# One core, HGRN2 outer-product attention followed by an activation MLP: the work of all engines put in a new order

## The chip, the cores and the metric

The kernel runs on one core of a Trainium2 chip. A core has a matrix engine (PE), a vector engine (DVE), an activation engine (ACT), a general engine (POOL), and queues that start DMAs (SP issues nearly all of them here). Each engine runs its own instructions strictly in the order in which they stand in its queue, and waits on semaphores for what the others deliver. The metric is the device time of one execution in microseconds, the median of several runs.

## The reference

The first half is a gated linear recurrence over 768 positions for 4 batches of 8 heads with 48 channels; the second half is a two-layer MLP with the activation h · erf(softplus(h)).

```
f = 1.0 / (1.0 + np.exp(-f_logit))
for t in range(S):
    state = f[:, :, t, :, None] * state + np.einsum('bhd,bhe->bhde', k[:, :, t], v[:, :, t])
    y[:, :, t] = np.einsum('bhd,bhde->bhe', q[:, :, t], state)
x = y.transpose(0, 2, 1, 3).reshape(B * S, H * D)      # 3072 x 384
h = x @ w_in                                           # 384 -> 2048
sp = np.maximum(h, 0.0) + np.log1p(np.exp(-np.abs(h)))
g = h * erf(sp)
out = g @ w_out                                        # 2048 -> 384
```

## The kernel before

The recurrence is cut into 24 chunks of 128 positions (6 for each batch), each in two halves of 64. Two chunks make a block of 256 tokens, so that the MLP runs over 12 blocks, each with 4 groups of 512 hidden channels.

A program of 1770 short tokens in the string STEPS says in which order all of this is issued. A token is a step's name, its numbers, sometimes the engine (a, v or g for ACT, DVE or POOL), and behind an @ the buffer that it takes. For chunk g: `f q k v` load; `cl ex ln` make log decays (DVE, ACT, ACT); `d` sums them (PE); `e` turns sums into decays (ACT, two instructions); `qd kd` scale q and k (DVE); `tq tk` or `tx` transpose both on PE; `aq ak` copy the transposes out; `ds` and `sc` are PE's state products and scores; `m` and `s` mask the scores (on DVE, or for chunks 3 to 9 by a copy on ACT and a select on POOL); `st` updates the running state on DVE for each half; `sp` copies the state to the operand of the next half; `y` is PE's output product for each half, and `x` copies the chunk to the block's input xT. For block b and group i: `h` is half a group's hidden product (6 matmuls of 128x256), `c` copies the group out of PSUM, `ae ax aw ah` are ACT's four functions, `at au am` DVE's three products, `ka kb kt` (ACT, DVE, DVE) split the result in three parts, and `o` is 4 matmuls of 128x384 that project one part. `ro rp so` gather a block's rows and store them.

The weights arrive in 16 pieces (`p`) and are rounded by seven steps each (`r`, step 0 on ACT and six on DVE); pieces 0 to 7 are w_in, and a hidden half p needs piece p. The four groups of w_out are split in parts by `kc` (ACT), `ku kD kM` (DVE). Block 0 is projected with plain w_out; the parts are needed from block 1 on, and lie in the memory that block 0's activations used.

Within an engine the order is that of the tokens and of nothing else. PSUM is four pairs of banks (@0 to @3 on PE's steps), and the activations share 13 slots of [128, 1024] (@0 to @12). A step that takes a buffer waits until its last reader is done. In the listings below a name such as pair_3385 is one use of a PSUM pair, early_m_110 the second half of plain w_out, form_c, form_d and form_m its parts, h, e, x, ga, gb, gs the activation slots.

The change touches STEPS, `form_d`, `copy_x`, `copy_h`, and the tiles called early, which were all made at the start. The engine of `sp`, `ak` and `v` was already a letter in the token; `x`, `c` and `kD` had a fixed one.

Of the kernel before, what the change touches and what calls it, by code (L numbers as in the profile page):

```python
# [79 lines left out]
def kernel(  # L80
# [133 lines left out]
    early = {n: parts.tile([P, PAIR], FP32, name=f"early_{n}", tag=n) for n in ("c0", "c1", "d0", "d1", "m0", "m1")}  # L214
    formed = {}

    def plain(ft, n=1):
        pair, at = divmod(ft * d_model, PAIR)
        return early[f"m{pair}"][:, at : at + n * d_model].rearrange("p (a w) -> p a w", w=d_model)
# [67 lines left out]
    def load_piece(i):  # L287
# [7 lines left out]
        raw = None if wpe == 1 else early[home[:2]][:, at : at + 2 * PIECE].bitcast(U32)  # L295
# [51 lines left out]
    def flat_form(t, gi):  # L347
        return form(t, gi).rearrange("p j c -> p (j c)")
# [261 lines left out]
    def copy_x(g):  # L610
        blk, j = divmod(g, CPB)
        if blk not in xTs:
            xTs[blk] = work.tile([P, n_k, TB], FP32, name="xT", tag="xT")
        nc.scalar.copy(out=xTs[blk][:, :, j * P : (j + 1) * P], in_=yts[g][:])
# [130 lines left out]
    def pads(_):  # L745
# [6 lines left out]
        f0 v0 k0 q0 f1 in0 ms0 zb0@0 p0 q1 cl0 ex0 k1 ln0 v0_0_0g v1 z5 d0@1 v0_0_1g f2 v0_1_1g  # L752
        e0 v0_1_0g p1 v2 kd0 z3 to0@1 qd0 p2 tk0@2 ta0 k2 cl1 tq0 ex1 q2 ak0a ds0 f3 aq0 st0 p3
        st1 sp0g ln1 v3 z2 sc0 r0_0 d1@2 p4 sp1g m0_0_1 m0_1_1 p5 e1 m0_0_0 r0_1 f4 z1 y0_0@3
        r0_2 to1@2 qd1 m0_1_0 kd1 z2 tq1@1 v1_0_0g ta1 r0_3 v1_0_1g q3 y0_1 v1_1_0g aq1 r0_4 k3
        tk1 v1_1_1g cl2 r0_5 f5 x0 ds1 ex2 r0_6 ak1a ln2 z2 sc1 st2 d2@1 st3 r1_0 sp2g p6 m1_0_0
        e2 p7 m1_1_1 sp3g m1_0_1 v4 m1_1_0 z3 y1_0@3 r1_1 v2_0_1g y1_1 r1_2 v2_1_0g to2@2 r1_3
        v2_1_1g x1 w3 v2_0_0g ta2 h0_0@0 r1_4 r2_0 r1_5 r2_1 kd2 r2_2 k4 tk2@3 qd2 r1_6 q4 ds2
        ak2a tq2 cl3 v5 st4 ex3 h0_1 r2_3 ln3 sp4g aq2 r2_4 r2_5 r3_0 r2_6 sc2 c0_0 r3_1 d3@3
        m2_0_0 ax0_0@0 m2_1_1 h0_2@0 f6 m2_0_1 m2_1_0 r3_2 r3_3 e3 r3_4 f7 y2_0@1 r3_5 r4_0 y2_1  # L760
        r3_6 to3@3 ae0_0@1 ta3 x2 st5 h0_3 r5_0 w4 r4_1 sp5g r4_2 aw0_0@2 r5_1 r4_3 qd3 c0_1
        r4_4 tq3@2 q5 kd3 ae0_1@3 r4_5 ds3 k5 tk3 aq3 v6 st6 cl4 sp6g ak3a r4_6 ex4 sc3 r5_2
        h0_4@2 p8 r5_3 r5_4 m3_0_0 m3_0_1 r5_5 m3_1_0 m3_1_1 s3_0 r6_0 r5_6 s3_1 ln4 st7 h0_5 p9
        r6_1 r7_0 sp7g r6_2 r6_3 r7_1 y3_0@3 r7_2 c0_2 r7_3 y3_1 d4@0 x3 w5 r6_4 d5@2 e4 r6_5
        h1_0@3 e5 r7_4 qd4 kd4 q6 r7_5 k6 tx4@2 r6_6 f8 to4@0 aq4 to5@1 r7_6 h1_1 ak4v ta4 ta5
        cl6 p10 qd5 ex6 p11 at0_0 ds4 sc4 c1_0@4 q7 v7 st8 m4_0_0 h0_6@3 m4_0_1 kd5 f9 sp8g
        m4_1_0 st9 m4_1_1 ln6 au0_0 s4_0 ax0_1@0 s4_1 h0_7 k7 sp9g r8_0 at0_1 ah0_0 y4_1@0 r8_1
        r8_2 c0_3 y4_0 r8_3 tx5@2 ms6 w6 x4 aw0_1@0 r8_4 h1_2@0 ak5v aq5 r8_5 r8_6 ax0_2@2 ds5
        am0_0 p12 r9_0 sc5 d6@2 v8 m5_0_0 h1_3 st10 m5_0_1 m5_1_0 r9_1 m5_1_1 sp10g e6 r9_2 r9_3
        s5_1 ae0_2@1 tt6 qd6 h1_4@2 r10_0 kd6 r9_4 c1_1@5 s5_0 r10_1 r10_2 r10_3 y5_0@0 r10_4  # L770
        y5_1 r10_5 tx6@1 x5 r9_5 w7 h1_5 aq6 ak6v r9_6 r10_6 p13 h1_6@1 c1_2@6 au0_1 k8 p14
        r11_0 at0_2 aw0_2@0 q8 r11_1 h1_7 ax0_3@2 r11_2 r11_3 ah0_1 r11_4 r11_5 r12_0 sc6@2
        am0_1 c1_3@7 ds6 d7@0 v9 o0_0_0@3 m6_0_0 st12 m6_0_1 f10 r12_1 m6_1_0 sp12g m6_1_1 r12_2
        e7 r12_3 s6_0 ae0_3@3 qd7 s6_1 h2_0@0 kd7 tt7 st13 r12_4 sp13g r12_5 r11_6 y6_0@2 y6_1
        r12_6 h2_1 x6 au0_2 r13_0 r14_0 r13_1 p15 r13_2 ah0_2 w8 tx7@2 r14_1 r14_2 c2_0@0 o0_0_1
        r14_3 aq7 ak7v q9 am0_2 aw0_3@8 k9 h2_2@2 r13_3 f11 ae1_0@1 r13_4 r14_4 r13_5 ds7@0
        r14_5 sc7 v10 h2_3 st14 m7_0_0 m7_0_1 at0_3 m7_1_0 sp14g m7_1_1 s7_0 au0_3 ax1_0@2
        o0_1_0 s7_1 r13_6 c2_1@9 r14_6 ah0_3 cl8 r15_0 am0_3 y7_0@2 ex8 y7_1 r15_1 o0_1_1 w9
        r15_2 r15_3 x7 r15_4 ln8 r15_5 aw1_0@3 h2_4@2 r15_6 at1_0 ae1_1@8 au1_0 o0_2_0 ax1_1@2
        st15 cl10 ah1_0 sp15g at1_1 aw1_1@3 h2_5 am1_0 aw1_2@2 au1_1 ka1_0@1 d8@0 ah1_1 o0_2_1  # L780
# [6 lines left out]
        kD3 ax2_0@12 kb1_2@10 au1_3 o1_2_0_0 c3_0@6 o1_2_0_1 kM2 ah1_3 o1_2_1_0 f12 h3_2@2
        aw2_0@11 kt1_2@5 qd9 kd9 q11 am1_3 h3_3 k11 at2_0 ae2_1@2 ka1_3@3 au2_0 tx9@3 ax2_1@12
        o1_2_0_2 kM3 o1_2_1_1 aq9 o1_2_1_2 ak9v ah2_0 o1_3_0_0 kb1_3@5 ds9@3 aw2_1@10 sc9 v12
        st18 o1_3_1_0 c3_1@7 kt1_3@11 sp18g o1_3_0_1 m9_0_0 o1_3_1_1 m9_0_1 am2_0 m9_1_0  # L790
        o1_3_0_2 m9_1_1 s9_0 ro1 o1_3_1_2 at2_1 ka2_0@8 s9_1 h3_4@1 au2_1 ae2_2@11 ax2_2@12
        kb2_0@5 h3_5 ah2_1 kt2_0@10 aw2_2@0 am2_1 rp1 y9_0@2 ae2_3@2 y9_1 at2_2 so1 c3_2@3
# [12 lines left out]
        ah3_3 f15 h4_3 ae4_0@9 am3_3 aw4_0@7 at4_0 ka3_3@4 sc11@2 au4_0 ds11 c4_1@12 o3_2_0_0
        v14 m11_0_0 o3_2_0_1 ah4_0 m11_0_1 o3_2_0_2 m11_1_0 m11_1_1 ax4_1@7 y11_0@1 st22
        o3_2_1_0 kb3_3@10 sp22g ae4_1@11 o3_2_1_1 kt3_3@0 o3_2_1_2 aw4_1@5 y11_1 am4_0 o3_3_0_0
        x11 w13 o3_3_0_1 at4_1 ka4_0@9 h4_4@1 au4_1 kb4_0@7 ah4_1 h4_5 kt4_0@5 am4_1 o3_3_0_2
        cl14 c4_2@1 o3_3_1_0 ax4_2@11 o3_3_1_1 h4_6@1 ae4_2@4 ro3 at4_2 ka4_1@10 h4_7 aw4_2@11
        kb4_1@3 ex14 au4_2 d12@3 o3_3_1_2 c4_3@11 o4_0_0_0@2 kt4_1@0 e12 o4_0_0_1 ah4_2  # L810
        o4_0_0_2@1 rp3 tt12 o4_0_1_0 qd12 h5_0@0 kd12 ax4_3@9 am4_2 ae4_3@12 h5_1 ka4_2@4 at4_3
# [332 lines left out]
```

## Time and profile before

| | us |
|---|---|
| median of 3 runs | 616.17 (615.49 to 618.18) |
| the profiled execution | 618.82 |
| its span | 617.1 |
| PE busy | 584.0 (95%) |
| DVE busy | 481.7 (78%) |
| ACT busy | 444.8 (72%) |
| POOL busy | 86.5 (14%) |

The span runs from the first to the last instruction of the profiled execution, which is 2.65 us longer than the median. Two stages differ. Up to about 200 us the weights are rounded while the first chunks and blocks run, and DVE is the busiest engine; from there PE is busy almost without a break to its last matmul at 609 us. A row of the timeline gives the start, the time, the engine, the line, the operation with its output and inputs, the number of instructions merged, and in brackets the idle time ahead of it with what ended it. PE's times within a row of several matmuls overlap with those of the next row, so that PE's pace is read from start to start. A matmul of 32-bit operands shows as two records.

### The profile page before, as it was taken

Reading aid. Unit: us, or ns where it says so; the run is one execution under the profiler, and the core shown is the slowest. Engines: PE = TensorE matmul, PEld = TensorE weight load, DVE = VectorE, ACT = ScalarE, POOL = GpSimd, SP = SyncE. Lnnn points to the kernel's source line nnn. Section 1 sums busy time; section 2 is a strip of 40 time slices with the busy share of each in tenths; the row PEclk is TensorE's granted clock in tenths of the full one; section 3 lists DMA queues with packets and bytes.
Section 4 is the critical chain, followed back from the end, with each engine's and each line's share of the span. In section 5 each row is a group of like instructions: output and inputs, shape, how many; then the busy total and the mean of one; then the engine's idle time right before and its main releaser. Section 6 shows DMA issues by size and latency. Waiting matters only on the chain.

```text
span 617.1 us, 14290 instructions
## 1 busy us (share of the span) xinstructions
PE 584.0 (95%) x5885; PEld 501.3 (81%) x5885; DVE 481.7 (78%) x603; ACT 444.8 (72%) x524; POOL 86.5 (14%) x133
## 2 busy tenths in 40 slices
PE   7897989899799999999999999999999999999995
PEld 6676867666588798888888888888888888889994
DVE  4989879999968989966867678569567778566783
ACT  4476586679768898879685786786898584575881
POOL 3203230223503200200001101100100101200000
PEclk9988989999989999999999999999999999999998
DMA  9986666411122112402132125113522121010000
GB/s 236 268 200 155 164 147 155 109 34 17 49 35 45 41 32 34 83 9 54 25 80 51 27 44 86 28 40 53 105 51 40 29 53 14 2 27 1 0 27 30
DMA packets 153095, 41.38 MB, mean 67 GB/s; under 512 B 144832, under 2 KB 147904, under 8 KB 153024
## 3 DMA queue, kind: packets, MB, share of 16 engines
q1 hardware_dynamic: 150944, 40.01, 29.8%
q8 instruction: 48, 0.79, 0.6%
q10 hardware_dynamic: 2080, 0.39, 0.3%
q14 instruction: 23, 0.19, 0.1%
HBM read 35.59 MB, written 4.72 MB: 65 GB/s over the span
## 4 chain that ended last, share of the span: by engine, by line
PE 75%; DVE 13%; ACT 5%; issue 3%; POOL 1%; SPq 1%; DMA 0%; DVEq 0%; ACTq 0%; POOLq 0%
PE pair L627 33%; PE pair L703 28%; PE pair L604 4%; PE pair L541 2%; DVE e L176 2%; PE pair L480 2%; PE pair L553 2%; DVE qA L578 1%; PE pair L427 1%; PE pair L561 1%; DVE early_m L341 1%; DVE state L522 1%; ACT qA L576 1%; ACT x L171 1%; PE pair L471 1%
## 5 line engine op out<-in xcount | busy, mean ns | idle before, releaser
L627 PE MATMUL pair<-xT,w_in_sb 128*128 128x256 f32 x1152 | 266.7, 387 | 7.4 <-ACT kd L436 2.5
L627 PEld LDWEIGHTS pair<-xT,w_in_sb 128*128 128x128 f32 x1152 | 220.1, 193 | 41.9 <-ACT kd L436 4.0
L176 DVE SCALAR_TENSOR_TENSOR e<-x,e 128x1024 f32<-128x1024 f32 x96 | 117.3, 1224 | 29.2 <-ACT e L168 19.5
L132 POOL COPY sv<-state 48x192 f32<-48x192 f32 x88 | 61.5, 699 | 457.8 <-DVE state L523 327.8
L171 ACT ACTIVATE x<-h,serf_bias 128x1024 f32<-128x1024 f32 x88 | 100.3, 1145 | 5.1 <-PE pair L703 1.6
L703 PE MATMUL pair<-form_c,ga 128*128 128x384 f32 x352 | 81.1, 352 | 1.3 <-DVE rows L717 1.3
L703 PE MATMUL pair<-form_m,gs 128*128 128x384 f32 x352 | 80.0, 350 | 0.0
L703 PE MATMUL pair<-form_d,gb 128*128 128x384 f32 x352 | 77.2, 341 | 0.0
L655 ACT ACTIVATE e<-e 128x1024 f32<-128x1024 f32 x48 | 50.7, 1057 | 28.5 <-DVE e L176 28.1
L659 DVE TENSOR_TENSOR h<-h,e 128x1024 f32<-128x1024 f32 x44 | 54.0, 1228 | 19.9 <-ACT e L655 19.7
L671 DVE TENSOR_TENSOR gb<-h,ga 128x1024 fp32r<-128x1024 f32 x44 | 54.5, 1239 | 14.2 <-ACT ga L666 10.4
L703 PEld LDWEIGHTS pair<-form_m,gs 128*128 128x128 f32 x352 | 62.4, 190 | 3.5 <-issue 2.1
L634 ACT COPY h<-pair 128x1024 f32<-128x1024 f32 x44 | 44.4, 1009 | 28.7 <-PE pair L627 25.9
L703 PEld LDWEIGHTS pair<-form_c,ga 128*128 128x128 f32 x352 | 60.5, 188 | 5.2 <-issue 2.3
L703 PEld LDWEIGHTS pair<-form_d,gb 128*128 128x128 f32 x352 | 61.9, 188 | 1.4 <-DVE gs L678 0.3
L666 ACT ACTIVATE ga<-h 128x1024 fp32r<-128x1024 f32 x44 | 46.3, 1053 | 20.0 <-DVE h L659 19.6
L678 DVE SCALAR_TENSOR_TENSOR gs<-ga,gb 128x1024 fp32r<-128x1024 f32 x44 | 54.1, 1230 | 3.5 <-PE pair L703 1.9
L168 ACT ACTIVATE e<-h 128x1024 f32<-128x1024 f32 x44 | 46.1, 1048 | 6.0 <-DVE h L659 3.0
L604 PEld LDWEIGHTS pair<-qA,sv 128*32 128x32 f32 x1536 | 26.1, 112 | 18.8 <-issue 6.4
L604 PE MATMUL pair<-qA,sv 128*32 128x64 f32 x1536 | 32.1, 225 | 9.6 <-POOL qA L585 5.1
L494 ACT COPY qA<-pair 64x512 f32<-64x512 f32 x48 | 27.8, 580 | 10.4 <-PE pair L480 5.0
L522 DVE TENSOR_TENSOR state<-pair,state 112x192 f32<-112x192 f32 x40 | 14.2, 355 | 24.1 <-PE pair L553 16.1
(92 smaller groups left out, 572.6 us busy)
## 6 DMA issues: line engine op xcount, KB each, us to landing
early_d<-in_moe_w_out_dram SPq DMA_DIRECT2D x8, 768.0 KB, 4.9
qn<-in_q_dram SPq DMA_DIRECT2D x24, 192.0 KB, 3.2
out_dram<-rows SPq DMA_DIRECT2D x12, 384.0 KB, 2.5
kn<-in_k_dram SPq DMA_DIRECT2D x23, 192.0 KB, 3.3
vt<-in_v_dram SPq DMA_DIRECT2D x23, 192.0 KB, 3.4
sv<-in_v_dram SPq DMA_DIRECT2D x84, 48.0 KB, 2.5
lt<-in_f_logit_dram SPq DMA_DIRECT2D x80, 48.0 KB, 2.4
early_m<-in_moe_w_in_dram SPq DMA_DIRECT2D x4, 768.0 KB, 6.2
```

The lines of the kernel that those rows point to most:

```text
L132: (engine.copy if engine is nc.scalar else engine.tensor_copy)(out=out, in_=in_)
L168: nc.scalar.activation(out=dst[:], in_=h, func=AF.Exp)
L171: nc.scalar.activation(out=dst[:], in_=h, func=AF.Tanh, bias=serf_bias[:, i : i + 1], scale=SERF_KAB[i][0])
L176: nc.vector.scalar_tensor_tensor(out=e[:], in0=x[:], scalar=SERF_KAB[i][2], in1=e[:], op0=ALU.add, op1=ALU.mult)
L604: nc.tensor.matmul(y[M * i : M * (i + 1), kt, half(c)], lhsT=sv[:, r, c, a, o : o + M], rhs=qA[:, r, a, half(c)], start=(first and n == 0) ...
L627: nc.tensor.matmul(hts[blk, gi][:, j, :], lhsT=w_in_sb[:, kt, ft * P : (ft + 1) * P], rhs=xTs[blk][:, kt, :], start=(kt == 0), stop=(kt == ...
L655: nc.scalar.activation(out=e[:], in_=e[:], func=AF.Tanh, scale=SERF_C)
L659: nc.vector.tensor_tensor(out=h, in0=h, in1=es.pop((blk, gi))[:], op=ALU.mult)
L666: nc.scalar.activation(out=gps_[blk, gi][0][:], in_=hs[blk, gi], func=AF.Copy, scale=KAPPA)
L671: nc.vector.tensor_tensor(out=gps_[blk, gi][1][:], in0=hs[blk, gi], in1=a[:].bitcast(FP32), op=ALU.subtract)
L678: nc.vector.scalar_tensor_tensor(out=gps_[blk, gi][2][:], in0=a[:].bitcast(FP32), scalar=1.0 / PART, in1=b[:].bitcast(FP32), op0=ALU.mult, ...
L703: nc.tensor.matmul(ots[blk, acc][:, tt, 0:d_model], lhsT=lhs.rearrange("p (j t) -> p j t", j=FG)[:, j, tt * P : (tt + 1) * P], rhs=rhs, st ...
```

## The change

The tokens of STEPS stand in another order, with other buffers behind the @, and four kinds of copies carry a letter for their engine: `c` (42 on ACT, 6 on DVE; all 48 on ACT before), `x` (20 on ACT, 4 on DVE; all 24 on ACT before), `kD` (4 on DVE, as before), and `v` (8 on POOL, 4 on ACT; all 12 on POOL before). Of the copies that had a letter already, `sp` goes from 44 on POOL to 28 on POOL, 10 on ACT and 6 on DVE, and `ak` from 4 on ACT and 20 on DVE to 2 and 22. The filler matmuls `z` go from 18 to 12. Nothing that is computed changes otherwise. The early tiles are made when they are first named.

```
-    early = {n: parts.tile([P, PAIR], FP32, name=f"early_{n}", tag=n) for n in ("c0", "c1", "d0", "d1", "m0", "m1")}
-    formed = {}
+    earlies, formed = {}, {}
+
+    def early(n):
+        if n not in earlies:
+            earlies[n] = parts.tile([P, PAIR], FP32, name=f"early_{n}", tag=n)
+        return earlies[n]
...
-    def form_d(gi):
+    def form_d(gi, engine):
+        if engine is nc.scalar:
+            nc.scalar.activation(out=flat_form("d", gi), in_=flat_plain(gi), func=AF.Copy, scale=PART)
+            return
...
-    def copy_x(g):
+    def copy_x(g, engine):
...
-        nc.scalar.copy(out=xTs[blk][:, :, j * P : (j + 1) * P], in_=yts[g][:])
+        copy_by(engine, xTs[blk][:, :, j * P : (j + 1) * P], yts[g][:])
...
-    def copy_h(blk, gi, n=None):
+    def copy_h(blk, gi, engine, n=None):
         hs[blk, gi] = h_home(blk, gi, n)
-        nc.scalar.copy(out=hs[blk, gi], in_=hts.pop((blk, gi)).rearrange("p j t -> p (j t)"))
+        copy_by(engine, hs[blk, gi], hts.pop((blk, gi)).rearrange("p j t -> p (j t)"))
...
-        f0 v0 k0 q0 f1 in0 ms0 zb0@0 p0 q1 cl0 ex0 k1 ln0 v0_0_0g v1 z5 d0@1 v0_0_1g f2 v0_1_1g
+        f0 f1 q0 k0 p0 in0 ms0 zb0@0 v0 f3 cl0 ex0 q1 cl1 ln0 f2 ex1 z6 d0@1 k1 ln1 v1 d1@2 e0
```

Three places show how rows move. The first is PE where the first hidden product comes (L627 before, L634 after; the lines of the changed kernel stand 4 to 8 lower). L541 and L548 are state products, L553 and L560 scores, L471 and L478 transposes. Before:

```order
L604 MATMUL pair_392<-qA,sv_91 32x64 x32
L561 MATMUL pair_429<-ident,dp_99 128x2 x4
L627 MATMUL pair_443<-xT,w_in_sb 128x256 x6
L471 MATMUL pair_457<-ident,kd_97 128x128 x4
L541 MATMUL pair_429<-vt_89,kd_97 64x48 x16
L471 MATMUL pair_457<-ident,qd 128x128 x4
L627 MATMUL pair_443<-xT,w_in_sb 128x256 x6
L553 MATMUL pair_429<-qA,kT 64x64 x16
```

The same stretch of PE in the changed kernel:

```order
L568 MATMUL pair_455<-ident,dp_100 128x2 x4
L548 MATMUL pair_371<-vt_89,kd_97 64x48 x16
L548 MATMUL pair_455<-vt_87,kd_98 64x48 x16
L560 MATMUL pair_371<-qA,kT 64x64 x16
L478 MATMUL pair_523<-ident,kd_98 128x128 x4
L478 MATMUL pair_523<-ident,qd 128x128 x4
L611 MATMUL pair_550<-qA,sv_90 32x64 x32
L560 MATMUL pair_455<-qA,kT 64x64 x16
L634 MATMUL pair_613<-xT,w_in_sb 128x256 x12
```

The first hidden product moved behind the state products and scores of chunks 2 and 3; before, chunk 2's state products stood behind a half of it.

The second place is DVE where the second half of w_out is split: L354 before and L358 after are `ku`, which waits for `kc` on ACT. From a state update of chunk 8 on, before:

```order
L522 TENSOR_TENSOR state_103<-pair_1641,state_102 112x192
L523 TENSOR_TENSOR state_103<-state_103,Tall 112x192
L354 TENSOR_TENSOR early_m_110<-form_c_1723,early_m_110 128x1536
L659 TENSOR_TENSOR h<-h,e 128x1024
L354 TENSOR_TENSOR early_m_110<-form_c_1723,early_m_110 128x1536
L359 TENSOR_SCALAR form_d_1817<-early_m_110 128x1536
```

And after, from behind the splitting of the first half (form_d_1677) on:

```order
L666 TENSOR_TENSOR h<-h,e 128x1024
L366 TENSOR_SCALAR form_d_1677<-early_m_126 128x1536
L678 TENSOR_TENSOR gb<-h,ga 128x1024
L371 TENSOR_TENSOR form_m_1728<-form_c_1623,form_d_1677 128x1536
L176 SCALAR_TENSOR_TENSOR e<-x,e 128x1024
L463 TENSOR_TENSOR kd_98<-kn_95,kd_98 128x8x48
L456 TENSOR_TENSOR qd<-qn_93,dp_100 128x8x48
L371 TENSOR_TENSOR form_m_1728<-form_c_1623,form_d_1677 128x1536
L358 TENSOR_TENSOR early_m_171<-form_c_1757,early_m_171 128x1536
```

Before, both `ku` of the second half stood close behind the state update; after, the whole splitting of the first half and five other steps stand between.

The third place is PE in a late block, from the state products of chunk 14 to its output products (L604 and L611). Before:

```order
L541 MATMUL pair_3385<-vt_89,kd_97 64x48 x16
L553 MATMUL pair_3385<-qA,kT 64x64 x16
L703 MATMUL pair_3150<-form_c_1723,ga 128x384 x4
L703 MATMUL pair_3150<-form_d_1817,gb 128x384 x4
L604 MATMUL pair_3439<-qA,sv_90 32x64 x32
```

After:

```order
L548 MATMUL pair_3246<-vt_89,kd_97 64x48 x16
L560 MATMUL pair_3246<-qA,kT 64x64 x16
L710 MATMUL pair_2983<-form_m_1833,gs 128x384 x8
L634 MATMUL pair_3222<-xT,w_in_sb 128x256 x6
L710 MATMUL pair_2930<-form_c_1757,ga 128x384 x4
L710 MATMUL pair_2930<-form_d_1795,gb 128x384 x8
L611 MATMUL pair_3335<-qA,sv_90 32x64 x32
```

Two projections stood between the scores and the output products; now five and a hidden half do.

More of the change, by code (lines that the diff above doesn't have):

```diff
@@ L231, in h_home @@
             pair, at = divmod(H_HOMES.index((blk, gi)), 3)
-            return early[("c0", "c1", "d0", "d1")[pair]][:, at * FG * TB : (at + 1) * FG * TB]
+            return early(("c0", "c1", "d0", "d1")[pair])[:, at * FG * TB : (at + 1) * FG * TB]
         return slot(n, "h")[:]
@@ L757 @@
[L757 to L768, printed above, removed]
@@ L787 @@
[L787 to L792, printed above, removed]
@@ L805 @@
[L805 to L810, printed above, removed]
```

249 lines of the change are left out of this document (137 added, 112 removed).

## The prediction

> **What bounds the kernel now.** The page comes first, for the shares of the whole; then the busy times on both sides of 196.5 us, a cut explained below.
>
> ```profile
> span 617.1 us, 14290 instructions
> PE 584.0 (95%) x5885; PEld 501.3 (81%) x5885; DVE 481.7 (78%) x603; ACT 444.8 (72%) x524; POOL 86.5 (14%) x133
> ```
>
> ```profile
> core 0: us, PE busy (x) PEld busy (x) DVE busy (x) ACT busy (x) POOL busy (x), PEclk, DMA share, GB/s
> 0.00:196.50 196.50, 174.63 (x1956) 139.01 (x1956) 168.01 (x238) 134.76 (x183) 49.51 (x74) 0.95 0.54 127
> 196.50:609.30 412.80, 409.12 (x3931) 362.28 (x3929) 312.36 (x363) 309.99 (x342) 37.03 (x60) 1.00 0.20 39
> ```
>
> Behind the cut PE is busy 409.12 of 412.80 us at full clock, and DVE only 312: PE's own work sets the time there. Ahead of it DVE is busy 168.0 of 196.5 us, more than any compute queue but PE, and PE's granted clock is 0.95. The timelines of DVE and PE show the cut itself, and PE's last matmul.
>
> ```profile
> 195.27 1.22 DVE L678 SCALAR_TENSOR_TENSOR gs<-ga,gb 128x1024 fp32r<-128x1024 f32 x1
> 196.62 1.58 PE L703 MATMUL pair<-form_m,gs 128*128 128x384 f32 x8
> 609.23 0.27 PE L738 MATMUL pair<-ident,low 128*1 128x128 f32 x1
> ```
>
> The gs that ends at 196.49 is `kt1_3`, the last activation part of block 1; PE starts on it 0.13 us later (`o1_3_0_2`). So the span is four terms: DVE's work up to `kt1_3` (168.0), DVE's waits up to there (28.5), PE from `o1_3_0_2` to its end (609.2 - 196.6 = 412.6), and 7.6 us in which the last rows are added and stored (617.1 less 609.5). The new order keeps these four and changes each of the first three. I work against this execution (618.82 us, 2.65 above the median of the runs) and take the difference off the median.
>
> **Work ahead of the cut.** I counted the DVE steps ahead of `kt1_3` in both orders: they are the same steps, but for three copies of kT (chunks 0, 1, 2) that were on ACT. On PE, the steps from `o1_3_0_2` on are the same but for two `o` more and one `d` less. The prices:
>
> ```profile
> L132 DVE COPY kT<-pair 128x512 f32<-128x512 f32 x20 | 13.8, 688 | 7.1 <-ACT qA L494 5.3 <-PE pair L480 1.8
> 538.85 0.87 PE L703 MATMUL pair<-form_m,gs 128*128 128x384 f32 x4
> 539.65 0.56 PE L427 MATMUL pair<-lt,tri 64*64 64x192 f32 x8
> 540.13 0.96 PE L703 MATMUL pair<-form_c,ga 128*128 128x384 f32 x4
> 540.93 0.85 PE L703 MATMUL pair<-form_d,gb 128*128 128x384 f32 x4
> 541.63 0.85 PE L703 MATMUL pair<-form_m,gs 128*128 128x384 f32 x4
> ```
>
> Three copies at 0.688 less the overlap of neighbours (0.61 from start to start, as at 69.70) are +1.8 us. An `o` takes 0.70 (540.93 to 541.63), a `d` 0.48 (539.65 to 540.13): 2 x 0.70 - 0.48 = +0.9. So far **+2.7 us**, the wrong way: nothing has been taken off DVE where DVE is the bound.
>
> **Waits ahead of the cut.** DVE's waits up to 196.5, by what ended them, the ones on which the change bears:
>
> ```profile
> DVE early_m L354 <- ACT form_c L351: 4.9, 2, 4.4
> DVE kd L456 <- ACT kd L436: 3.8, 1, 3.8
> DVE state L522 <- PE pair L541: 2.6, 1, 2.6
> DVE state L520 <- PE pair L541: 2.4, 1, 2.4
> DVE Tall L567 <- PE pair L561: 0.9, 1, 0.9
> DVE qA L578 <- PE pair L553: 0.7, 1, 0.7
> ```
>
> The 3.8 is the first chunk's chain from load to decays and stays. The 2.4, 0.9 and 0.7 (4.0 together) are chunk 0 on its way through PE, with nothing else in DVE's queue. The new order puts six or more ready steps there (two rounding steps and a kT copy ahead of the second qd, then more rounding). They need the first weight piece, whose landing the profile only gives as a median of 6.2 us. I take 2.5 of the 4.0; the ends are 0 (piece late) and 4.0.
>
> The 2.6 comes from PE:
>
> ```profile
> 28.72 5.47 PE L627 MATMUL pair<-xT,w_in_sb 128*128 128x256 f32 x12
> ```
>
> Half a hidden group, at about half pace, stood ahead of chunk 2's state products. In the new order the state products and scores of chunks 2 and 3 stand ahead of the first hidden half (the first listing), so this wait goes. What is late next is PE itself, whose first hidden product then has, by my count of the steps at their start-to-start times, 27.2 us of PE steps ahead of it instead of 22.3; that it costs DVE little is a choice, and so I take 2.0; ends 0 and 2.6.
>
> The 4.4 is a chain over POOL:
>
> ```profile
> 160.99 4.39 POOL L132 COPY sv<-state 48x192 f32<-48x192 f32 x2 [14.35 <-DVE state L523]
> 165.33 4.18 POOL L585 TENSOR_SCALAR_AFFINE_SELECT qA<-qA 64x512 f32<-64x512 f32 x2
> 169.47 0.74 POOL L132 COPY sv<-state 48x192 f32<-48x192 f32 x2
> 169.57 1.92 PE L604 MATMUL pair<-qA,sv 128*32 128x64 f32 x60 [3.22 <-POOL qA L585]
> 171.54 0.48 ACT L614 COPY xT<-pair 128x384 f32<-128x384 f32 x1 [5.48 <-PE pair L604]
> 173.43 1.76 DVE L354 TENSOR_TENSOR early_m<-form_c,early_m 128x1536 f32<-128x1536 f32 x1 [4.43 <-ACT form_c L351]
> ```
>
> The state copies and selects of chunk 8 end at 169.5, y follows, then x on ACT, then form_c in ACT's queue behind x, then DVE: 12.5 us from the state update at 160.8 to DVE's restart. All of it is still on POOL and ACT in the new order, and form_c stands behind one `c` and one `e` more (1.0 + 2 x 0.48 of ACT rows). But DVE's next `ku` has moved: from the same state update it now has two `ku` and two `kM` (1.68 each), two `kD` (0.87), three products (1.14), a state update (0.66), kd and qd (0.47 each) ahead of it, 13.5 us, against the 12.5 + 1.9 = 14.4 that the chain needs. The wait falls from 4.4 to about 0.9: -3.5; ends 0 and -4.4.
>
> On that chain a page speaks against the change. By the Trainium skill, GPSIMD Engine Reference, 1. Specifications, POOL's SBUF interfaces are shared with VectorE, and contend with DVE instructions that have two SBUF inputs. This trace agrees: two copies took 4.39 us beside DVE's two-input products and 0.74 at 169.47, when DVE was idle. By that rule the copies stay slow under the two-input `ku` and `kM` now packed around them, and the wait shrinks by 3.5 only; at the pace of 169.47 it would vanish, and the sum would be 0.9 lower.
>
> New waits. ACT gets four table loads more ahead of `kt1_3` (11 against 7), two of them around blocks 0 and 1's last tanh.
>
> ```profile
> L171 ACT ACT_TABLE_LOAD x9 | 11.5, 1283 | 0.1
> 150.00:200.00 50.00, 45.37 (x414) 38.50 (x413) 41.72 (x39) 38.23 (x47) 13.47 (x8) 0.93 0.23 45
> ```
>
> They are 4 x 1.28 = 5.1 us of ACT, in a stage where ACT was busy 38.2 of 50: it has room, but a load just ahead of a tanh delays DVE's product. I take half, 2.6; ends 0 and 5.1. Sum of waits: -2.5 - 2.0 - 3.5 + 2.6 = **-5.4**, between -11.0 and +5.1.
>
> **PE behind the cut.** Two prices. First, whenever PE changes between the big steps (`h`, `o`) and the small ones of the attention, the step ahead and the step behind each take 0.10 longer: 538.85 to 539.65 is 0.80 and 540.13 to 540.93 is 0.80, against 0.70 for 540.93 to 541.63. So a stretch of small steps costs 0.20 beside its own work. From `o1_3_0_2` on there were 61 such stretches; the new order has 49. 12 x 0.20 = **-2.4**.
>
> Second, the output products wait for masks and state copies. A free one, a held one, and the first and last held ones of nine:
>
> ```profile
> 373.38 1.10 PE L604 MATMUL pair<-qA,sv 128*32 128x64 f32 x64
> 374.41 0.96 PE L703 MATMUL pair<-form_c,ga 128*128 128x384 f32 x4
> ...
> 341.80 1.06 PE L604 MATMUL pair<-qA,sv 128*32 128x64 f32 x36
> 343.01 0.64 PE L604 MATMUL pair<-qA,sv 128*32 128x64 f32 x28
> 343.58 0.96 PE L703 MATMUL pair<-form_m,gs 128*128 128x384 f32 x4
> ...
> 232.96 1.21 PE L604 MATMUL pair<-qA,sv 128*32 128x64 f32 x64 [0.50 <-DVE qA L578]
> 555.36 1.35 PE L604 MATMUL pair<-qA,sv 128*32 128x64 f32 x64 [0.36 <-POOL sv L132]
> ```
>
> Free, a chunk's `y` takes 1.03 (373.38 to 374.41); at 341.80 it took 1.78. Of the 14 chunks from 10 on, nine are held, by 0.5 to 0.85 each, 6.0 together, and five are free. What separates them is PE's work between the scores and `y`: the free ones had 3.3 us or more, the held ones 1.4 to 2.8. In the new order (third listing) nine chunks have 3.3 or more, and five (13, 19, 20, 22, 23) have 2.1 to 2.8, where the held ones lost some 0.55: 5 x 0.55 = 2.7. So **-3.3**, between 0 (a copy on a busy engine holds them instead) and -6.0.
>
> **The moved copies themselves.** No row shows `c` on DVE. The nearest:
>
> ```profile
> L717 DVE TENSOR_TENSOR rows<-rows,pair 128x768 f32<-128x768 f32 x11 | 10.5, 951 | 3.5 <-PE pair L738 2.3 <-ACT rows L714 1.0
> L576 ACT COPY qA<-pair 64x256 f32<-64x256 f32 x28 | 10.3, 367 | 6.9 <-DVE state L522 4.7 <-PE pair L553 1.0 <-DVE state L520 0.8
> L132 POOL COPY sv<-state 48x192 f32<-48x192 f32 x88 | 61.5, 699 | 457.8 <-DVE state L523 327.8 <-DVE state L520 70.7 <-PE pair L703 56.6
> ```
>
> With 0.95 for three quarters of the size and 2 x 0.69 for two kT copies, it lies between 0.95 and 1.38, where ACT takes 1.01; I take 1.24. All six stand behind the cut, where DVE has 100 us of room, and the PSUM pair is next taken after 2.1 us of PE steps or more: nothing, or 0.4 each if DVE is late. A state copy of 0.70 on POOL is some 0.37 on ACT; that is part of the -3.3. The four `x` on DVE have 2 us or more of PE ahead of their `h`, the four `v` on ACT stand ahead of the first y, hidden behind chunk 0's scores. The six fillers fewer (z) are 2.6 us of PE that nothing waited for.
>
> **Sum.** +2.7 - 5.4 - 2.4 - 3.3 = **-8.4 us**: 610.4 for an execution like the profiled one, 616.17 - 8.4 = **607.8** as a median.
>
> **Rivals.** *A: the waits only change place.* Every wait that I strike out is replaced by one as long, since DVE's steps depend on PE and ACT all along. For it: the 25 us of waits have seven or more different releasers. Against it: the three that I remove have named fillers. Then +2.7 - 2.4 - 3.3 = -3.0: **613.2**. *B: the new order is slower.* ACT's four more table loads reach DVE in full, ahead of `kt1_3`: +5.1, no old wait saved, and the held `y` find their state copies behind ACT's and DVE's long steps, so that only the stretches gain: +2.7 + 5.1 - 2.4 = +5.4, **621.6**. It decides if ACT loses its room in that stage, 50 - 38.2 - 5.1 = 6.7 us, to waits for PE; the one at 171.54 was 5.5. *C: everything hides.* All ends on the good side: +2.7 - 11.0 - 2.4 - 6.0 = -16.7, **599.5**; against it stand 14 chunks that would all have to be free.
>
> **Chances.** My forecast 0.50, A 0.25, B 0.15, C 0.10. The range that leaves out two in ten runs from between C and the forecast, 601, to between A and B, 619.5. Within 0.5% means 613.1 to 619.2, about what a measurement of this kernel can tell from no change. Faster: 0.46 of the forecast, 0.11 of A, all of C: 0.67. Slower: most of B: 0.13. The rest, 0.20, is no change.
>
> **What would show it.** In the changed kernel's DVE timeline `kt1_3` (a gs of line 685) ends near 193 us (196.5 + 1.8 - 5.4); the second pair of `ku` (line 358) waits 1 us or less; the state updates of chunks 0 and 2 wait less than a microsecond for PE. From there PE takes about 408 us (412.6 + 0.9 - 2.4 - 3.3), with five held `y` or fewer. I am wrong if `kt1_3` ends after 197 us, above all with ACT's rows ahead of DVE's waits (B), or if PE's part is no shorter than 412 us.

## The result, and the profile after

| | before | changed |
|---|---|---|
| median | 616.66 us (4 runs) | 632.32 us (632.00 to 633.19, 4 runs) |
| ratio | | 1.0255 (95%: 1.0229 to 1.0281) |
| profiled execution | 618.82 us | 632.46 us |

The change makes the kernel 2.6% slower; the forecast was 607.8, in a range from 601.0 to 619.5. The first lines of the page of the changed kernel:

```profile
span 630.5 us, 14178 instructions
PE 581.5 (92%) x5873; PEld 504.9 (80%) x5873; DVE 485.3 (77%) x627; ACT 448.7 (71%) x540; POOL 114.8 (18%) x97
```

POOL's copies of a state ahead of the cut (up to the end of `kt1_3`) as a group, with its busy time and the mean of one in ns, in the kernel before:

```profile
L132 POOL COPY sv<-state 48x192 f32<-48x192 f32 x35 | 30.1, 860 | 138.9 <-DVE state L523 115.3 <-DVE state L520 22.6
```

And in the changed kernel:

```profile
L132 POOL COPY sv<-state 48x192 f32<-48x192 f32 x29 | 59.8, 2063 | 91.0 <-DVE state L530 79.6 <-DVE state L527 10.5
```

POOL has fewer instructions than before (97 against 133) and is busy longer (114.8 us against 86.5). Its copies of a state take 2.06 us in the mean ahead of the cut, where they took 0.86. The busy times ahead of the cut in the changed kernel (stretch, its length, then PE, PEld, DVE, ACT and POOL, then PE's granted clock, the share of the DMA engines and GB/s):

```profile
0.00:212.24 212.24, 174.68 (x1939) 140.13 (x1940) 162.22 (x241) 139.93 (x192) 88.66 (x64) 0.90 0.50 117
```

Its timeline, at the end of `kt1_3` and at PE's first and last matmul behind it:

```profile
211.02 1.22 DVE L685 SCALAR_TENSOR_TENSOR gs<-ga,gb 128x1024 fp32r<-128x1024 f32 x1
213.28 0.87 PE L710 MATMUL pair<-form_m,gs 128*128 128x384 f32 x4
622.57 0.27 PE L745 MATMUL pair<-ident,low 128*1 128x128 f32 x1
```

By the four terms of the prediction: DVE's work up to `kt1_3` 162.2 (168.0 before), its waits up to there 50.0 (28.5), PE from `o1_3_0_2` to its last matmul 409.3 (412.6), with 1.0 between `kt1_3` and this (0.1), and the tail 7.9 as before. So the loss lies ahead of the cut, in DVE's waits: 21.5 us more. The longest of them, by what ended them (36 to 212.24 us):

```profile
DVE kd L463 <- ACT kd L443: 26.1, 2, 20.6
DVE kT L132 <- PE pair L487: 3.6, 1, 3.6
```

One wait of 20.6 us is more than the 15.7 us by which the median grew. PE's granted clock is lower in this stretch too (0.90 against 0.95), but this does not explain the loss: experiment 6 below reaches the cut 22 us sooner at 0.92. The timelines of POOL, DVE and PE around the wait:

```profile
37.54 24.55 POOL L132 COPY sv<-state 48x192 f32<-48x192 f32 x2 [0.34 <-DVE state L530]
...
48.90 0.55 DVE L335 TENSOR_SCALAR early_d<-w_in_sb 128x768 uint32<-128x768 uint32 x1
49.37 0.55 DVE L322 TENSOR_SCALAR w_in_sb<-w_in_sb 128x768 f32<-128x768 f32 x1
...
60.54 0.94 DVE L345 TENSOR_TENSOR w_in_sb<-early_d,w_in_sb 128x768 f32<-128x768 f32 x1
82.09 0.56 DVE L463 TENSOR_TENSOR kd<-kn,kd 128x384 f32<-128x384 f32 x1 [20.61 <-ACT kd L443]
62.76 0.43 PE L611 MATMUL pair<-qA,sv 128*32 128x64 f32 x4 [18.05 <-POOL qA L592]
```

Two copies of 48x192, 0.74 us where nothing is in their way, took 24.55 us: they ended at 62.09, just behind DVE's run of rounding steps, which ended at 61.48. The select of chunk 3 stands behind them on POOL, chunk 3's `y` on PE waits for the select (18.05), `x` on ACT for `y` (17.22), and so on to `kd` on DVE. So DVE first keeps POOL out, and then stands still for 20.6 us because POOL was late. POOL is kept out for over 6 us three times more. The selects at 119.88 and 171.94 then held a `y` for 3.64 and 5.87 us; the copies at 151.26 held none. POOL's rows for these:

```profile
119.88 6.89 POOL L592 TENSOR_SCALAR_AFFINE_SELECT qA<-qA 64x512 f32<-64x512 f32 x2
151.26 14.51 POOL L132 COPY sv<-state 48x192 f32<-48x192 f32 x2 [11.84 <-DVE state L530]
171.94 9.86 POOL L592 TENSOR_SCALAR_AFFINE_SELECT qA<-qA 64x512 f32<-64x512 f32 x2
```

How DVE's steps follow each other is the point to read. From 48.90 on each step begins before the one ahead has ended (49.37, where that one ends at 49.45): neighbours belong to two different pieces of the weights, and neither reads the other's result. In the kernel before, the six DVE steps of a piece stood mostly one behind the other, each reading what the one ahead had written. Two such steps there:

```profile
42.68 0.56 DVE L322 TENSOR_SCALAR w_in_sb<-w_in_sb 128x768 uint32<-128x768 uint32 x1
43.27 0.96 DVE L327 SCALAR_TENSOR_TENSOR w_in_sb<-early_m,w_in_sb 128x768 uint32<-128x768 uint32 x1
```

The first ends at 43.24, and the second begins 0.03 later.

### The profile page after: what moved, and what is told of

Read it like the earlier page. It is cut to its first block, busy times and chain, and to the rows that moved or that the text cites. A ratio compares the mean times of both kernels' runs of the same rounds, so it can differ in the third digit from the quotient of the medians.

```text
span 630.5 us, 14178 instructions
## 1 busy us (share of the span) xinstructions
PE 581.5 (92%) x5873; PEld 504.9 (80%) x5873; DVE 485.3 (77%) x627; ACT 448.7 (71%) x540; POOL 114.8 (18%) x97
## 4 chain that ended last, share of the span: by engine, by line
PE 79%; POOL 7%; issue 5%; DVE 3%; ACT 3%; DMA 1%; SPq 0%; DVEq 0%; POOLq 0%; ACTq 0%
PE pair L634 35%; PE pair L710 31%; POOL sv L132 5%; PE pair L611 4%; PE pair L548 2%; POOL qA L592 2%; PE pair L487 2%; PE pair L560 2%; PE pair L434 1%; PE pair L568 1%; PE pair L478 1%; DMA lt<-in_f_logit_dram 1%; ACT qA L501 1%; DVE state L529 0%; DVE state L530 0%
## 5 line engine op out<-in xcount | busy, mean ns | idle before, releaser
L634 PE MATMUL pair<-xT,w_in_sb 128*128 128x256 f32 x1152 | 271.9, 389 | 1.1 <-DVE state L529 0.7
L634 PEld LDWEIGHTS pair<-xT,w_in_sb 128*128 128x128 f32 x1152 | 220.6, 194 | 33.6 <-issue 1.6
L132 POOL COPY sv<-state 48x192 f32<-48x192 f32 x56 | 78.7, 1405 | 355.3 <-DVE state L530 286.4
L710 PEld LDWEIGHTS pair<-form_c,ga 128*128 128x128 f32 x352 | 62.1, 189 | 4.5 <-issue 1.7
L611 PE MATMUL pair<-qA,sv 128*32 128x64 f32 x1536 | 31.2, 236 | 34.6 <-POOL qA L592 31.4
L611 PEld LDWEIGHTS pair<-qA,sv 128*32 128x32 f32 x1536 | 26.4, 120 | 42.9 <-POOL qA L592 33.4
L132 ACT COPY h<-pair 128x1024 f32<-128x1024 f32 x38 | 38.4, 1011 | 30.0 <-PE pair L634 26.0
L463 DVE TENSOR_TENSOR kd<-kn,kd 128x384 f32<-128x384 f32 x24 | 13.4, 557 | 27.8 <-ACT kd L443 27.6
```

What stands on the lines that cost most here:

```text
L132: (engine.copy if engine is nc.scalar else engine.tensor_copy)(out=out, in_=in_)
L611: nc.tensor.matmul(y[M * i : M * (i + 1), kt, half(c)], lhsT=sv[:, r, c, a, o : o + M], rhs=qA[:, r, a, half(c)], start=(first and n == 0) ...
L634: nc.tensor.matmul(hts[blk, gi][:, j, :], lhsT=w_in_sb[:, kt, ft * P : (ft + 1) * P], rhs=xTs[blk][:, kt, :], start=(kt == 0), stop=(kt == ...
L710: nc.tensor.matmul(ots[blk, acc][:, tt, 0:d_model], lhsT=lhs.rearrange("p (j t) -> p j t", j=FG)[:, j, tt * P : (tt + 1) * P], rhs=rhs, st ...
```

## The experiments

**Theory S** (POOL starves): POOL gets in where DVE runs dry for a moment, which happens where a step reads the result of the one ahead of it. The new order interleaves independent steps, so that DVE never runs dry, and POOL starves.

**1. The same order, rounding piece by piece.** Only the 33 rounding steps in DVE's long run change places among themselves:

```
- r3_2 r1_5 r3_3 r1_6 r3_4 r2_1 r3_5 r2_2 r3_6 r2_3 r4_1 r2_4 r4_2 r2_5 r4_3 r2_6 r4_4 r5_1 ...
+ r1_5 r1_6 r3_2 r3_3 r3_4 r3_5 r3_6 r2_1 r2_2 r2_3 r2_4 r2_5 r2_6 r4_1 r4_2 r4_3 r4_4 r4_5 ...
```

> The changed kernel; only the 33 rounding steps on DVE between the state copy of chunk 3 and the next kd are put piece by piece (each step behind the one whose result it reads), where the change had interleaved two pieces. Theory S (POOL starves: its two state copies at 37.54 took 24.55 us because DVE ran independent steps without a break until 61.48; a step that reads the result of the one ahead lets DVE run dry for a moment, and POOL gets in): the two copies take under 5 us, PE's wait of 18.05 us ahead of y falls under 4, DVE's rounding gets 2 to 4 us longer (33 steps x about 0.1), and the time falls by 12 to 17 us, to 615 to 620. Rival O (it is the order of the steps on PE and ACT: DVE has nothing else to do until y is done, POOL only looks late): the gap stays, 632 +- 2. Rival T (steps with two SBUF inputs shut POOL out in whatever order): the copies still take over 20 us, 632 +- 2.

Measured: 620.99 us, 11.3 less than the changed kernel (ratio to before 1.0056, 1.0035 to 1.0077). In this run, POOL's two copies and, further on, a select of chunk 5, then two of DVE's steps and the `y` behind that select:

```profile
38.03 1.56 POOL L132 COPY sv<-state 48x192 f32<-48x192 f32 x2 [0.34 <-DVE state L530]
85.42 9.19 POOL L592 TENSOR_SCALAR_AFFINE_SELECT qA<-qA 64x512 f32<-64x512 f32 x2 [3.68 <-ACT qA L583]
...
45.03 0.55 DVE L322 TENSOR_SCALAR w_in_sb<-w_in_sb 128x768 f32<-128x768 f32 x1
45.62 0.56 DVE L326 TENSOR_SCALAR w_in_sb<-w_in_sb 128x768 uint32<-128x768 uint32 x1
94.96 2.32 PE L611 MATMUL pair<-qA,sv 128*32 128x64 f32 x64 [5.50 <-POOL sv L132]
```

24.55 became 1.56, with the same instructions on every engine. Each step now begins 0.03 or 0.04 after the one ahead ended (45.03 + 0.55 = 45.58, next at 45.62). That costs DVE 0.12 a step (0.59 from start to start instead of 0.47), 4 us for the 33, which S had allowed for. The gain is a little under the 12 to 17 that S expected. One new loss stands in the trace: the selects of chunk 5, which took 2.38 us in the changed kernel, took 9.19 here, and a `y` waited 5.50 us behind them. O and T, both at 632, fall.

**2 and 3. Chunk 3 off POOL, in two steps.** First only the copy (`sp6g` becomes `sp6a`); then chunk 3's masks on DVE too:

```
-    SELECT = range(3, 10)
+    SELECT = range(4, 10)
...
- sp6g
+ sp6a
- s3_0
- s3_1
```

> The changed kernel; only the state copy that took 24.55 us on POOL (sp6) is given to ACT. Theory S: the copy takes 0.7 us on ACT, but POOL's select of chunk 3, next in its queue, stands beside the same unbroken run of DVE steps and ends no sooner than 62 us, so PE's wait stays at 15 us or more and the time within 2 us of 632. Rival C (only that copy is slow, by its shape): the select is done by 43 us, PE's wait is gone, 615 to 620.

> The changed kernel; the state copy sp6 on ACT, and chunk 3's masks made by DVE's products as for chunks 0 to 2 instead of ACT's copies and POOL's selects (4 DVE steps of 0.42 more, 4 ACT copies of 0.37 and 2 selects fewer), so that POOL has nothing to do in the stretch from 38 to 62 us. Theory S: PE waits under 4 us ahead of chunk 3's y, and the time falls by 13 to 18 us, to 614 to 619. Rival O: the gap stays in place, 630 to 633.

Measured: 630.30 us (ratio 1.0241, 1.018 to 1.0302) with the copy alone, and 617.35 (0.9977, 0.9943 to 1.001) with the masks too. The runs of the second scatter: nine from 611.5 to 619.1, and a tenth of 623.6. In the first of the two, POOL's next instruction takes the place of the copy:

```profile
40.54 21.93 POOL L592 TENSOR_SCALAR_AFFINE_SELECT qA<-qA 64x512 f32<-64x512 f32 x2 [3.59 <-ACT qA L583]
61.81 0.43 PE L611 MATMUL pair<-qA,sv 128*32 128x64 f32 x4 [18.11 <-POOL qA L592]
```

So it is not that copy but POOL in that stretch. With chunk 3 freed, PE still waits for POOL ahead of five `y` up to 230 us, 19.8 us in all:

```profile
PE pair L611 <- POOL qA L592: 14.3, 4, 5.9
PE pair L611 <- POOL sv L132: 5.5, 1, 5.5
```

**4 and 5. POOL beside DVE, alone.** Two kernels that only run POOL's copies beside runs of DVE steps of 128x768 (or 128x512 from PSUM). In the first, the copies begin together with the run; in the second a small DVE step in the middle of the run releases them:

```
+ for i in range(6):
+     step(i)
+ nc.vector.tensor_tensor(out=src[0:112, :], in0=src[0:112, :], in1=zero[0:112, 0:192], op=ALU.subtract)
...
+ for i in range(N):
+     step(i)
```

> No part of the reference is computed (the output is zeros). Eight stretches: four POOL copies of 48x192 beside 24 DVE steps each, of one kind per stretch: none; one SBUF input, independent; one SBUF input, each reading the last; two SBUF inputs, independent; two, each reading the last; one and two in turn, independent; one PSUM and one SBUF input; PSUM copies. Theory S: the four copies take about 1.4 us beside nothing and beside the two PSUM kinds; beside the independent one-input and two-input steps the first does not end before the 24 steps do (11 and 21 us); beside the steps that read the last one's result each copy ends within one or two steps. Rival T: beside two inputs they wait to the end however the steps depend. Rival H (the port is held for one instruction only): beside every kind a copy waits one step at most, under 6 us for the four.

> No part of the reference is computed (the output is zeros). As the measurement of POOL beside DVE, where the copies began together with the first DVE step and got in at its end, but here the two POOL copies (48x192) are released by a small DVE step in the middle of a run of 6 + 24 steps, as a state copy is in the kernel. Stretches two by two: one SBUF input, independent; two inputs, independent; one and two in turn, independent; two inputs, each reading the last. In the second of each two, POOL's output tile was last read by ACT, so that the copy has a second semaphore to wait for, as in the kernel. Theory S: in the independent stretches at least one copy waits to the end of the run (over 8 us), in the chained ones none over 2 us. Rival H (one step at most): none over 2 us anywhere, and then what shuts POOL out in the kernel is not the unbroken run alone.

POOL's rows in the first kernel, the stretches in the order of the expectation:

```profile
7.54 1.55 POOL L68 COPY got<-src 48x192 f32<-48x192 f32 x4 [7.10 <-DVE src L66]
9.73 2.46 POOL L68 COPY got<-src 48x192 f32<-48x192 f32 x4 [0.64 <-DVE src L66]
22.02 2.45 POOL L68 COPY got<-src 48x192 f32<-48x192 f32 x4 [9.84 <-DVE src L66]
36.71 4.05 POOL L68 COPY got<-src 48x192 f32<-48x192 f32 x4 [12.23 <-DVE src L66]
58.60 4.05 POOL L68 COPY got<-src 48x192 f32<-48x192 f32 x4 [17.84 <-DVE src L66]
...
99.95 1.56 POOL L68 COPY got<-src 48x192 f32<-48x192 f32 x4 [13.84 <-DVE src L66]
```

And in the second (one input, two, both in turn, and steps that read the last one's result):

```profile
10.83 11.79 POOL L75 COPY got<-src 48x192 f32<-48x192 f32 x2 [10.39 <-DVE src L71]
44.44 21.39 POOL L75 COPY got<-src 48x192 f32<-48x192 f32 x2 [6.22 <-DVE src L71]
98.46 16.59 POOL L75 COPY got<-src 48x192 f32<-48x192 f32 x2 [5.02 <-DVE src L71]
143.49 2.03 POOL L75 COPY got<-src 48x192 f32<-48x192 f32 x2 [6.83 <-DVE src L71]
```

The first kernel did not do what S expected: beside independent steps the four copies took 2.46 and 4.05 us, as beside dependent ones, so that POOL got in once a step (Rival H). The second did: released in the middle of a run, two copies took 11.79, 21.39 and 16.59 us beside independent steps, to the end of the run each time, and 2.03 beside steps with two inputs that read the last one's result. In a second stretch of each kind, where POOL's output had last been read by ACT, they took 11.79, 21.32, 16.52 and 1.96. Beside steps that read PSUM nothing is lost (1.56 against 1.55). So S holds for a request that comes into a running run, and a run that begins together with the request doesn't shut POOL out.

**6 and 7. POOL emptied up to the cut, in both orders.** State copies of chunks 3 to 9 on ACT, masks of chunks 3 to 9 by DVE's products:

```
-    SELECT = range(3, 10)
+    SELECT = range(0)
...
- sp6g sp8g sp9g sp10g sp12g sp13g sp14g sp15g sp16g sp17g sp18g sp19g
+ sp6a sp8a sp9a sp10a sp12a sp13a sp14a sp15a sp16a sp17a sp18a sp19a
```

> The changed kernel; POOL is freed of all that reads its shared operands in the first stage: the state copies of chunk 3 and of chunks 4 to 9 on ACT, the masks of chunks 3 to 9 by DVE's products (28 steps of 0.42, 11.8 us of DVE more; 28 ACT copies and 14 POOL selects fewer). With only chunk 3 freed (617.35) PE still waited 19.8 us ahead of y for POOL, in five places. Theory S: these go, DVE's mask products fill DVE's waits in part, and the time falls to 603 to 611, below the kernel before: the new order is a good one but for POOL. Rival D (DVE is the bound ahead of the projections, so that its work sets the time): 11.8 us more of DVE cost more than the waits were worth, 616 to 626.

> The kernel before, with the same engines for the same copies and masks as the run with an empty POOL: state copies of chunks 3 to 9 on ACT, masks of chunks 3 to 9 by DVE's products. In the kernel before PE waited only 5.1 us ahead of y for POOL in this stage. Theory S: POOL was no brake there, so DVE's 11.8 us more cost 4 to 10 us: 620 to 627, and the two orders stand 12 to 20 us apart, the other way round than as they were given. Rival G (an empty POOL helps any order): under 613.

Measured: **602.27 us** in the new order (ratio 0.9738, 0.9708 to 0.9767; S had set 603 to 611), 616.28 in the order before (0.9976, 0.9952 to 1.0). (There `sp7`, which the change had given to ACT, stayed on POOL.) The stretch ahead of the cut in the new order:

```profile
0.00:190.23 190.23, 171.17 (x1942) 137.49 (x1943) 171.18 (x265) 138.16 (x188) 12.87 (x31) 0.92 0.56 131
```

And its timeline at the cut and at the end:

```profile
189.00 1.23 DVE L685 SCALAR_TENSOR_TENSOR gs<-ga,gb 128x1024 fp32r<-128x1024 f32 x1
190.75 0.87 PE L710 MATMUL pair<-form_m,gs 128*128 128x384 f32 x4
595.53 0.27 PE L745 MATMUL pair<-ident,low 128*1 128x128 f32 x1
```

The cut comes at 190.2, 22 us sooner than in the changed kernel, although DVE has 28 mask products more: its work ahead of the cut is 171.2 us (162.2 in the changed kernel), its waits 19.1 (50.0). The same engines gain nothing in the order before, where `kt1_3` is this row:

```profile
194.35 1.22 DVE L678 SCALAR_TENSOR_TENSOR gs<-ga,gb 128x1024 fp32r<-128x1024 f32 x1
```

It ends at 195.6, against 196.5. The busy times up to there:

```profile
0.00:195.57 195.57, 175.89 (x1955) 139.47 (x1956) 173.54 (x261) 131.94 (x177) 14.11 (x41) 0.95 0.54 127
```

So with POOL emptied in both, the new order is worth 14.0 us (616.28 to 602.27), and the run in the new order stands 15.6 under the kernel before (617.88 in the same comparison). As given, with POOL in DVE's runs, the new order lost 15.7. Both rivals fall, and so does a part of S: I had expected the order before to lose 4 to 10. Two things cancelled in that run. DVE's work rose by 5.5 us (168.0 to 173.5), and its waits fell by 6.5 (28.5 to 22.0); the wait at `ku`, 4.4 before, was 0.5. That the work rose by less than the 11.8 of the mask products fits with the steps that POOL had slowed: 20 DVE steps ahead of the cut ran over 15% longer than the shortest of their form in these traces before (6.0 us in all), and 6 did here (0.6).

**8 and 9. Half of it each.** Only the state copies off POOL, or only the masks:

> Half of the run with an empty POOL (602.27): chunk 3 freed of POOL and the state copies of chunks 4 to 9 on ACT, but the masks of chunks 4 to 9 still by ACT's copies and POOL's selects. Theory S (any POOL instruction that reads is shut out by an unbroken DVE run): the selects still take 5 to 10 us each, PE still waits over 10 us ahead of y, 609 to 616. Rival C (the copies of 48 partitions are the ones that suffer): 600 to 605.

> The other half: masks of chunks 3 to 9 by DVE's products, no select left on POOL, but the state copies of chunks 4 to 9 on POOL as in the changed kernel (only sp6 on ACT). Theory S: fewer POOL instructions stand in DVE's runs, one or two of the copies still take over 5 us, and the time is between, 603 to 611. Rival C' (only the selects mattered): 600 to 604, and no copy over 3 us.

Measured: 604.07 us with the selects left on POOL (0.9804, 0.9775 to 0.9832), 609.13 with the copies left there (0.9891, 0.9851 to 0.993). The worst row of POOL ahead of the cut in the first:

```profile
112.62 6.12 POOL L592 TENSOR_SCALAR_AFFINE_SELECT qA<-qA 64x512 f32<-64x512 f32 x2 [10.59 <-issue]
```

And in the second, with the `y` behind it on PE:

```profile
121.67 8.77 POOL L132 COPY sv<-state 48x192 f32<-48x192 f32 x2 [10.11 <-DVE state L530]
130.08 1.47 PE L611 MATMUL pair<-qA,sv 128*32 128x64 f32 x32 [6.06 <-POOL sv L132]
```

Either kind can be shut out, but only some are, and which ones changes with small shifts of time. I had set 609 to 616 for the selects alone; it was 604, where rival C had it, since only this pair of selects took over 2 us, and one of 5.58 us at the cut itself. But C's reason, that the copies alone suffer, does not hold: selects were kept out for 6.12 us here and for 21.93 in experiment 2. Rival C' falls with the 8.77 of the second run.

**10. What freed the late `y`.** The run with POOL emptied, and the 13 state copies behind the cut that ACT and DVE had been given back on POOL (`sp30a` becomes `sp30g`, and so on):

> The run with an empty POOL in the first stage (602.27), with the 13 state copies of chunks 10 to 23 that the change had given to ACT and DVE back on POOL, where the kernel before had them. Question: what made the held y free behind the cut (all 14 take about 1.03 us in the changed kernel, where I had counted five held ones). Theory F (PE's work between scores and y): the chunks with 2.1 to 2.8 us there are held again by about 0.55 each, those with more are not, +2 to +4 us, 604 to 606. Rival E (any filler of 2 us hides a POOL copy): no y over 1.3 us, 601 to 604. Rival W (POOL was too slow everywhere): nine or more held, +6 or more.

Measured: 602.95 us (0.9793, 0.9759 to 0.9828). No `y` of these chunks is held: from its start to the next step they take 1.03 to 1.14 us, but for the last (1.28). A middle one:

```profile
448.40 1.19 PE L611 MATMUL pair<-qA,sv 128*32 128x64 f32 x64
449.52 0.96 PE L710 MATMUL pair<-form_c,ga 128*128 128x384 f32 x4
```

Rival E holds. The engines' letters are worth nothing there, and in this order 2.1 us of other work on PE are enough. In the order before, chunks with as much as 2.8 us were held, so this filler alone does not decide it; what else does was not tested.

**11 and 12. ACT's table loads.** The logarithms of a pair of chunks directly behind its exponentials, for chunks 8 and 10, and for all from 8 on (the second with the late copies on POOL):

```
- ex8 o0_0_1@3 at0_3 v10 p15 st14 q9 aw0_3@4 r13_1 sp14a k9 r14_1 y7_0@2 f11 r13_2 o0_0_0 r14_2 r13_3 ln8
+ ex8 ln8 o0_0_1@3 at0_3 v10 p15 st14 q9 aw0_3@4 r13_1 sp14a k9 r14_1 y7_0@2 f11 r13_2 o0_0_0 r14_2 r13_3
```

> The run with an empty POOL (602.27; PE starts the projection behind the cut at 190.75), with the logarithms of chunks 8 and 10 directly behind their exponentials on ACT, so that ACT changes its table 7 times ahead of the cut instead of 11, as in the kernel before. Question: the term +2.6 of the forecast (4 loads of 1.28 us, taken at half). Theory L (they reach DVE): the cut comes 2 to 5 us sooner, 597 to 600. Rival N (ACT has room, they cost nothing): within 1 us of 602.3. Rival B (the loads as forecast in the slower case) would need the whole 5.1.

> The run with an empty POOL in the first stage and the late state copies on POOL (602.95), with the logarithms of all pairs of chunks from 8 on directly behind their exponentials: 19 table loads instead of 31. Theory L: the 4 ahead of the cut bring 2 to 5 us, the 8 behind it nothing, since PE is busy there without a break: 598 to 601. Rival N: 602 to 604.

Measured: 603.64 us (0.9776, 0.9749 to 0.9803) and 606.62 (0.9827, 0.9804 to 0.9851). Neither brings anything: theory L falls (a gain of a microsecond would be lost in the scatter, since the runs of experiment 6 go from 599.9 to 605.0), and the second is some 3.7 us slower than its parent, for a reason that I did not look for (a longer stretch on ACT ahead of steps that wait is likely, but not shown).

## Why the prediction was wrong

**The step that failed.** "Sum of waits: -2.5 - 2.0 - 3.5 + 2.6 = **-5.4**, between -11.0 and +5.1." DVE's waits ahead of the cut grew by 21.5. For new waits the sum held the table loads only. I filled DVE's waits with ready steps and booked that as gain, without asking who had used those pauses; a new wait of 20.6 us behind POOL, at a place where the kernel before had none, was in no term and no rival. Yet I had the mechanism in hand: "By that rule the copies stay slow under the two-input `ku` and `kM` now packed around them, and the wait shrinks by 3.5 only". I used it as the duration of one row (4.39 us) in one chain. It is no duration. In the four cases here, POOL stayed out until DVE ran dry, so the price was what was left of DVE's run: 24.55, 14.51, 9.86 and 6.89 us. The price follows from the order, which is what the change alters; it can't be taken from the order before.

The listing of what moved could have shown it. Before, rounding steps of one piece mostly follow one another; in the changed kernel, the steps of two pieces alternate over 23 us without a step that reads PSUM, with a state copy and two selects on POOL beneath. The Trainium skill, SBUF — State Buffer, Who interferes with whom, states that the two engines share one port pair, as an exclusive lock that one holds for a whole instruction while the other is fully blocked (it names DVE steps with two SBUF inputs or in a two-port mode). The traces agree that POOL can be blocked, and not only slowed; but it was blocked for a whole run of DVE instructions, not for one (21.39 us, 24 steps, in experiment 5).

**Point by point.**

- Of the struck-out waits, two of three went. DVE's timeline of the changed kernel at the early chunks and at the second half's `ku`:

```profile
11.24 0.17 DVE L574 COPY Tall<-pair 128x8 f32<-128x8 f32 x1 [2.15 <-PE pair L568]
13.04 0.69 DVE L132 COPY kT<-pair 128x512 f32<-128x512 f32 x1 [0.58 <-PE pair L478]
19.56 0.69 DVE L132 COPY kT<-pair 128x512 f32<-128x512 f32 x1 [1.13 <-ACT qA L501]
21.16 0.17 DVE L574 COPY Tall<-pair 128x8 f32<-128x8 f32 x1 [0.46 <-PE pair L560]
31.32 0.17 DVE L574 COPY Tall<-pair 128x8 f32<-128x8 f32 x1 [0.34 <-PE pair L548]
32.55 0.36 DVE L529 TENSOR_TENSOR state<-pair,state 112x192 f32<-112x192 f32 x1 [0.60 <-PE pair L560]
...
188.70 1.75 DVE L358 TENSOR_TENSOR early_m<-form_c,early_m 128x1536 f32<-128x1536 f32 x1
193.51 1.75 DVE L358 TENSOR_TENSOR early_m<-form_c,early_m 128x1536 f32<-128x1536 f32 x1
```

  Chunks 0 and 1 on their way through PE: 4.3 us where it was 4.0 (I had 1.5; the wait only changed place, as rival A said). The state behind the first hidden half: 0.9 of 2.6 (I had 0.6). The second half's `ku`: nothing of 4.4 (I had 0.9). In all -5.8, where I had -8.0. But the chain behind the 4.4 did not go. I had counted chunk 9's `kd` among the ready steps ahead of `ku`; it needs `e` on ACT, which stands behind chunk 8's `x`, and so it waited for the same select and `y` (5.53 us at 186.09).
- New waits: I had 2.6 for table loads. Experiment 11 took four loads away with POOL emptied, and nothing came of it that stands out of the scatter; in the changed kernel itself it was not tried. In their place came POOL's: 20.6 and 5.5 at `kd`, and 3.6 at a kT copy whose transposes stood behind a `y` held by a select (`y` at 126.83).
- Work ahead of the cut: I had 169.8, and it was 162.2. The interleaving saves DVE 0.12 on each step that no longer waits for the one ahead, and fewer steps ran over 15% longer than the shortest of their form (15, by 3.0 us in all, against 20 by 6.0). A gain that I had not seen, and the other side of the loss.
- PE behind the cut: I had -4.8, and in the changed kernel it was -3.3, with 3.6 lost to POOL at the `y` of chunk 9. Without POOL (experiment 6) it was 404.8 against 412.6, -7.8. The term that was mis-sized is that of the held `y`: none of the five with 2.1 to 2.8 us of filler was held. With all of the 6.0 saved, +0.9 - 2.4 - 6.0 = -7.5.
- "Nothing has been taken off DVE where DVE is the bound": this was not so plain. PE was busy longer than DVE there (174.6 of 196.5 us), and in experiment 7 DVE's work rose by 5.5 us while the end of `kt1_3` went from 196.5 to 195.6. Since that run also took POOL's waits away, it does not show that DVE's work is free. I now read that stage as chains in which DVE, PE, ACT and POOL wait for each other; no run tests this by itself.
- Rival B gave the sign, and a third of the size (+5.4, where the median went up by 15.7), but by luck: its reason was the table loads, of which experiment 11 found no cost. The forecast of 607.8 would have been near, and on the high side, for the new order with POOL emptied: 602.3.

What stays open: what decides whether POOL gets in where DVE does not run dry. I counted in the traces of eight kernels (before, changed, experiments 1, 2, 3, 8, 9, 10) the POOL instructions that began under a DVE step which reads SBUF alone and is followed by another such. Where the follower began after the end of the first, 36 of 36 got in at that point. Where the two overlapped, 48 of the 60 that came after a pause of POOL were shut out, and 20 of the 84 that came directly behind another POOL instruction. One copy was shut out for 14 us in the changed kernel (151.26) and let in at the end of the same DVE step in experiment 2, with the same DVE steps around it and the same distance to their starts within 0.01 us.

## What to carry to other kernels

A helper that a busy engine can keep out lives on that engine's pauses, as POOL did on DVE's here. Whoever reorders work to fill the pauses of the busy engine should first list what the helper did in them, and price its work by the length of the new unbroken run, not by its old durations. And where a reordering fails, it is worth trying again with the helper's work taken off it: here the same order went from 632.3 to 602.3 us, 2.6% under the kernel before.

## What the runs showed that I had not expected

- A run of independent DVE steps keeps a POOL copy out for the whole run (21.39 us beside steps with two SBUF inputs, 11.79 beside those with one), if the copy is released in the middle of it; a copy that begins with the run gets in after the first step.
- A DVE step that reads the result of the one ahead begins 0.03 to 0.04 us after its end instead of 0.08 before: 0.12 us a step, and the opening for POOL.
- With POOL emptied, 28 mask products more on DVE, some 11.8 us by their usual time, cost the order before nothing (616.28 against 617.88 in the same comparison): DVE's work ahead of the cut rose by 5.5 us, and its waits fell by 6.5.
